# Low parts of block 0's FFN weights on GpSimd, the AV sum as one strided reduction, ten pair tiles, and a new order

## The chip, the cores and the metric

The kernel runs on one core of a Trainium2 chip. Its engines work side by side: TensorE (PE, matmuls; PEld are its weight loads), ScalarE (ACT), VectorE (DVE), GpSimd (POOL), and SyncE (SP), whose queue issues all transfers here. The metric is device time in microseconds (us), lower is better. The profile is of one execution; its span begins at the first and ends at the last recorded instruction.

## The reference

Everything is fp32; one sequence of 2048 positions, width 640, 32 heads of 20, FFN width 1728.

```python
H = 32; Dh = D // H; W, dil = 8, 2
qkv = (x @ wqkv)                       # x: layer-normed
idx = pos[:, None] - off[None, :]      # each position sees itself and 7 earlier ones, 2 apart
logits = jnp.einsum("bhsd,bhswd->bhsw", q, kg) * scale   # masked where idx < 0
attn = _softmax(logits, axis=-1)
o = jnp.einsum("bhsw,bhswd->bhsd", attn, vg)
h = x + o @ wo
g = _silu(ln(h) @ w_gate); u = ln(h) @ w_up
out = h + (g * u) @ w_down
```

## The kernel before

Positions are cut into four blocks of 512 (b = 0 to 3). Matmuls run on fp32r operands in three passes: each fp32 matrix is split into a high part (a rounded copy, made by ScalarE) and a low part (the rest, a subtraction), and high x high, low x high and high x low are added in PSUM. A low part is made by the helper `low`, on VectorE.

The stages are: QKV projections of all blocks (`qkv`, L691); attention on VectorE (`att_qk`, `att_exp`, `att_av`); output projection per block (`wo`, L888, and `wo3` for block 3, L1262); FFN of blocks 0 and 1 (`ffn`, `classic`: gate and up projections L976, down projections L991); FFN of blocks 2 and 3 together (`pair`), where a *pair tile* (`pair_tile`, L1164) takes a tile of 128 FFN columns through both blocks in a Winograd manner, 54 matmuls for what two classic tiles do in 2 x 30; at the end `products` (L1435), seven products in place of eight for the down projections of eight paired tiles.

The FFN has 14 tiles. `EARLY` says how many leading tiles blocks 2 and 3 take in the classic way (`ones` in `pair`, together with tile 13): with EARLY = 2 these are tiles 0, 1 and 13, eleven tiles are pair tiles, eight of those are *kept* for `products`. The classic tiles of block 2 are matmul work that does not need block 3, so it can run beside `wo3`.

Attention has 16 units (block, head group), two halves (`jp`) each. In a half, VectorE multiplies a window of keys with the queries into the buffer PROD (L755, 2560 elements per partition), reduces over the 20 head elements (L760), and later multiplies values with weights into PROD (L795), sums over the eight window places by halving three times in place (L804: 1280, 640, 320 elements), and transposes the result (L811). PROD is one buffer: each product waits for all readers of the one before.

The low parts of the FFN weights of block 0 are made by VectorE (`split`, L952: three subtractions of 640 per tile, from the loaded weights and their high parts, L957 and L942 on ScalarE), written to HBM (`lsc`) and loaded again for blocks 1 and 2. Products of FFN tiles come back through L1014 (ScalarE, silu), L1015 (VectorE, gate times up), L1005 and L1007 (split of the product), before the down matmuls.

The order of the work on each engine is not the program's: `Plan.add` records every operation with its reads and writes, and the table `ORDER`, worked out ahead by a planner from costs, says in which sequence the recorded operations are issued. Each row of it is (engine, number of the operation on that engine, how many). Every engine, SP's queue too, works its own sequence strictly in that order and waits by semaphores for what it needs from the others. `prio`, `cost` and `nbytes` in `P.add` have no effect beside a given `ORDER`.

GpSimd has little to do before the change: some memsets, among them empty operations that hold a place in the order.

Of the kernel before, what the change touches and what calls it, by code (L numbers as in the profile page):

```python
# [25 lines left out]
EARLY, NP = 2, 4  # L26
# [283 lines left out]
def dve(n):  # L310
    return 0.155 + 0.00104 * n
# [5 lines left out]
def pool(n):  # L317
    return 0.2 + 0.00218 * n
# [10 lines left out]
def program(tc, x_in, wqkv_in, wo_in, ffn_in, ffl_in, const_in, out):  # L329
# [8 lines left out]
    with tc.tile_pool(name="sb", bufs=1) as sb, tc.tile_pool(  # L338
# [107 lines left out]
        def low(n, fn, r, w, prio):  # L446
            P.add("DVE", dve(n), lambda: fn(V), r=r, w=w, prio=prio)
# [335 lines left out]
        def att_av(b, g, n, ko, vo, qo, lo, mo):  # L783
# [8 lines left out]
            for jp in range(2):  # L792
# [9 lines left out]
                def half(m, dst):  # L802
                    v = pq(PROD, 2560).rearrange("p (j w c) -> p j w c", j=2, w=W)
                    V.tensor_add(dst(v), v[:, :, 0:m, :], v[:, :, m : 2 * m, :])  # L804
# [833 lines left out]
```

## Time and profile before

| | us |
|---|---|
| median of 3 runs | 847.01 |
| lowest, highest | 845.8, 847.99 |
| profiled execution, its own time | 847.86 |
| its span | 845.8 |
| TensorE busy | 833.5 |
| VectorE busy | 753.7 |
| ScalarE busy | 431.9 |
| GpSimd busy | 2.8 |

The granted TensorE clock is 1.00 nearly throughout. Rows of groups give line, engine, operation, output<-input, shapes and count, then busy time and mean ns of one, then idle time of the engine just before and what ended it. Rows of waits give who waited for whom, us in total, times, longest.

### The profile page before, as it was taken

The page shows a single profiled execution, that of the slowest core. Times are in us where ns is not written, and L with a number is a line of the kernel's source. Part 1 is how long each engine was busy: PE and PEld are TensorE (multiplying, and loading weights), DVE is VectorE, ACT ScalarE, POOL GpSimd, SP SyncE. Part 2 cuts the span into 40 slices and gives each one's busy share as a digit, 9 for nine tenths or more (in the row PEclk, how much of TensorE's full clock was granted, in tenths as well). Part 3 has the DMA queues.
Part 4 walks back from the last instruction along what each step waited for, and adds up shares of the span by engine and source line. Part 5 has one row for each costly group of instructions (what it writes and reads, how often), then busy time and mean ns, then how long its engine had stood idle before and what let it go on. Part 6 is the DMA issues. An engine that isn't in the chain of part 4 may idle for free.

```text
span 845.8 us, 11075 instructions
## 1 busy us (share of the span) xinstructions
PE 833.5 (99%) x4037; PEld 713.4 (84%) x4037; DVE 753.7 (89%) x974; ACT 431.9 (51%) x804; POOL 2.8 (0%) x13
## 2 busy tenths in 40 slices
PE   8999999999999999999999999999999999999998
PEld 6888888889978788888888888888788888887998
DVE  6499999999998999999999999999986756667996
ACT  7755466253772443468345339467933232335550
POOL 0000000000000000000000000000000000000000
PEclk9999999999999999999999999999999999999999
DMA  7896978757779897679989989876322223268002
GB/s 256 224 246 172 283 203 236 217 142 227 187 216 282 271 283 235 222 218 275 328 265 299 283 278 283 247 268 241 120 90 75 88 82 100 81 227 323 1 33 93
DMA packets 89158, 173.35 MB, mean 205 GB/s; under 512 B 34464, under 2 KB 51200, under 8 KB 88464
## 3 DMA queue, kind: packets, MB, share of 16 engines
q1 hardware_dynamic: 89104, 172.66, 66.8%
q8 instruction: 31, 0.51, 0.2%
q14 instruction: 23, 0.19, 0.1%
HBM read 125.09 MB, written 47.16 MB: 204 GB/s over the span
## 4 chain that ended last, share of the span: by engine, by line
PE 78%; DVE 9%; DMA 8%; ACT 2%; issue 1%; SPq 1%; DVEq 0%; ACTq 0%
PE bank L691 18%; PE bank L976 18%; PE bank L1164 15%; PE bank L991 13%; PE bank L1435 6%; PE bank L888 5%; PE bank L1262 2%; DMA kv<-ksc 2%; DVE pq L795 1%; DMA pq<-qsc 1%; DMA vsc<-st 1%; DVE pq L755 1%; DMA lsc<-rb 1%; DVE rb L952 1%; DMA psc<-fa 1%
## 5 line engine op out<-in xcount | busy, mean ns | idle before, releaser
L976 PE MATMUL bank<-shb,rb 128*128 128x512 f32 x885 | 212.5, 390 | 1.9 <-DVE fa L1015 1.5
L976 PEld LDWEIGHTS bank<-shb,rb 128*128 128x128 f32 x885 | 165.1, 188 | 37.5 <-DVE fa L1015 2.4
L991 PE MATMUL bank<-rb,acts 128*128 128x512 f32 x464 | 122.5, 391 | 0.5 <-DVE acts L1009 0.5
L991 PEld LDWEIGHTS bank<-rb,acts 128*128 128x128 f32 x464 | 86.5, 188 | 18.4 <-DVE acts L1009 0.9
L755 DVE TENSOR_TENSOR pq<-kv,pq 128x2560 f32<-128x2560 f32 x32 | 90.2, 2820 | 6.4 <-DMA pq<-qsc 3.0
L804 DVE TENSOR_TENSOR pq<-pq 128x1280 f32<-128x1280 f32 (+2 forms) x96 | 89.4, 931 | 1.8
L795 DVE TENSOR_TENSOR pq<-kv,pq 128x2560 f32<-128x2560 f32 x32 | 90.2, 2820 | 0.7
L760 DVE TENSOR_REDUCE pq<-pq 128x128 f32<-128x2560 f32 x32 | 90.0, 2812 | 0.4
L698 ACT ACTIVATE st<-bank,fa 128x128 f32<-128x128 f32 (+3 forms) x120 | 50.5, 476 | 64.4 <-PE bank L691 37.7
L888 PE MATMUL bank<-ra 128*128 128x320 f32 x360 | 56.0, 309 | 0.0
L888 PEld LDWEIGHTS bank<-ra 128*128 128x128 f32 x360 | 54.3, 188 | 1.7 <-ACT fa L891 0.2
L691 PE MATMUL bank<-ra,sha 128*128 128x480 f32 (+2 forms) x240 | 54.4, 382 | 0.7 <-DVE sha L639 0.5
L691 PE MATMUL bank<-ra,shb 128*128 128x512 f32 (+1 forms) x240 | 52.5, 378 | 0.9 <-ACT st L698 0.9
L691 PE MATMUL bank<-rb,sha 128*128 128x512 f32 (+1 forms) x240 | 52.9, 379 | 0.0
L691 PE MATMUL bank<-rb,shb 128*128 128x512 f32 (+1 forms) x230 | 51.5, 379 | 0.0
L691 PEld LDWEIGHTS bank<-ra,shb 128*128 128x128 f32 x240 | 44.9, 188 | 7.8 <-ACT st L698 1.2
L691 PEld LDWEIGHTS bank<-ra,sha 128*128 128x128 f32 x240 | 44.3, 188 | 8.0 <-DVE sha L639 0.9
L691 PEld LDWEIGHTS bank<-rb,sha 128*128 128x128 f32 x240 | 44.8, 188 | 6.5
L691 PEld LDWEIGHTS bank<-rb,shb 128*128 128x128 f32 x230 | 42.9, 188 | 6.2
L957 ACT CAST rb<-fa 128x1280 fp32r<-128x1280 f32 (+1 forms) x32 | 38.9, 1215 | 17.9 <-DMA fa<-in_ffn_dram 14.4
L1014 ACT ACTIVATE fa<-bank 128x512 f32<-128x512 f32 x30 | 17.9, 598 | 51.1 <-PE bank L976 41.5
L952 DVE TENSOR_TENSOR rb<-fa,rb 128x640 fp32r<-128x640 f32 (+1 forms) x52 | 41.9, 814 | 1.1 <-ACT rb L957 1.1
(213 smaller groups left out, 1309.0 us busy)
## 6 DMA issues: line engine op xcount, KB each, us to landing
fa<-in_ffn_dram SPq DMA_DIRECT2D x33, 960.0 KB, 5.3
kv<-ksc SPq DMA_DIRECT2D x32, 440.0 KB, 6.2
kv<-vsc SPq DMA_DIRECT2D x32, 440.0 KB, 7.7
rb<-lsc SPq DMA_DIRECT2D x15, 640.0 KB, 6.4
lsc<-rb SPq DMA_DIRECT2D x13, 640.0 KB, 7.6
rb<-lsc SPq DMA_DIRECT2D x19, 320.0 KB, 4.4
ksc<-st SPq DMA_DIRECT2D x32, 160.0 KB, 3.5
pq<-qsc SPq DMA_DIRECT2D x16, 320.0 KB, 7.0
```

The lines of the kernel that those rows point to most:

```text
L691: T.matmul(banks[bk][:, 0:n], l, r_(wq(g, w, c) + shift, n), start=(p, c) == first_mm, stop=(p, c) == last_mm)
L698: P.add("ACT", act(m) + 0.06, lambda: A.activation(stage_t()[:, o : o + NJ * m].rearrange("p (t j c) -> p t j c", j=NJ, c=w)[:, :, j, :], ...
L755: P.add("DVE", dve(2560), lambda: V.tensor_tensor(pq(PROD, 2560).rearrange("p (j w c) -> p j w c", j=2, w=W), window(ko, 2 * jp), pq(qo + ...
L760: P.add("DVE", dve(2560), lambda: V.tensor_reduce(logits(lo)[:, :, 16 * jp : 16 * jp + 16].rearrange("p h n -> p n h"), pq(PROD, 2560).rea ...
L795: V.tensor_tensor(pq(PROD, 2560).rearrange("p (j n d) -> p j n d", j=2, d=DH), bass.AP(tensor=v.tensor, offset=v.offset, ap=[list(v.ap[0]) ...
L804: V.tensor_add(dst(v), v[:, :, 0:m, :], v[:, :, m : 2 * m, :])
L888: T.matmul(banks[bk][:, 0:320], l, r_(m, 320), start=p == 0 and c == 0, stop=p == 2 and c == NC - 1)
L952: low(640, lambda E, o=o: E.tensor_sub(ws(t, lo + o, 640)[p0:], fa[p0:, raw + o : raw + o + 640], ws(t, hi + o, 640)[p0:].bitcast(F32)), [ ...
L976: T.matmul(banks[bk], ws(wt, gu + 1280 * w + wid * c + col, 128), x(a, c), start=p == 0 and c == 0, stop=p == 2 and c == NC - 1)
L991: T.matmul(banks[k], l, m, start=first and p == 0, stop=stop and p == len(passes) - 1)
L1164: T.matmul(banks[bk], ws(wt, o + 2048 * w + 128 * k, 128), xv_[k](a), start=first and p == 0 and k == 0, stop=stop and p == 2 and k == n - ...
L1435: T.matmul(banks[bk0 + tp][:, 0:HN], v[:, 512 * a + 128 * tp : 512 * a + 128 * tp + 128], v[:, 1024 + HN * w : 1024 + HN * w + HN], start= ...
```

## The change

Four things change.

1. `low` gets a switch `aside`; `split` and `down_lo` pass it for block 0, so that the 41 subtractions of block 0's FFN weights are GpSimd's.
2. The AV sum, three halvings in PROD, becomes one VectorE reduction that reads PROD with the window place innermost (a step of 160 floats) and writes 320 sums into a free part of the query buffer; the transposition reads those.
3. After each of the 64 products a *token* is added on GpSimd: a copy of one element of PROD. It waits for the product, it does not hold back the reduction behind it, and the next product waits for it, since it reads PROD. In GpSimd's sequence it stands between the subtractions.
4. EARLY is 3: ten pair tiles in place of eleven, one classic tile more in block 2 and in block 3. The table `ORDER` is a new one.

```diff
-EARLY, NP = 2, 4
+EARLY, NP = 3, 4
...
 ORDER = (
-    (4, 2, 1), (4, 7, 1), (4, 4, 1), (2, 0, 1), (3, 1, 1), (3, 0, 1), (2, 1, 1), (1, 0, 1), (1, 10, 1), (2, 7, 1), (4, 3, 1), (2, 10, 1), (0, 0, 1), (4, 9, 1),
...
+    (4, 547, 1), (4, 552, 1), (4, 551, 1), (0, 833, 1), (2, 779, 1), (0, 828, 2), (2, 778, 1), (4, 546, 1), (4, 550, 1), (4, 549, 1),
...
-        def low(n, fn, r, w, prio):
-            P.add("DVE", dve(n), lambda: fn(V), r=r, w=w, prio=prio)
+        def low(n, fn, r, w, prio, aside=False):
+            if aside:
+                P.add("POOL", pool(n), lambda: fn(G), r=r, w=w, prio=prio)
+            else:
+                P.add("DVE", dve(n), lambda: fn(V), r=r, w=w, prio=prio)
...
+        def token():
+            P.add("POOL", 0.17, lambda: G.tensor_copy(f(LN + 122, 1), pq(PROD, 1)), r=[rpq(PROD, 1)], w=[rf(LN + 122, 1)], prio=20)
+
         def att_qk(jp, b, g, n, ko, vo, qo, lo, mo):
...
+            token()
             P.add("DVE", dve(2560), lambda: V.tensor_reduce(
...
-                def half(m, dst):
-                    v = pq(PROD, 2560).rearrange("p (j w c) -> p j w c", j=2, w=W)
-                    V.tensor_add(dst(v), v[:, :, 0:m, :], v[:, :, m : 2 * m, :])
-                for m in (4, 2):
-                    P.add("DVE", tt(320 * m), lambda m=m, half=half: half(m, lambda v: v[:, :, 0:m, :]),
-                          r=[rpq(PROD, 2560)], w=[rpq(PROD, 2560)], prio=20)
-                P.add("DVE", tt(320), lambda half=half: half(1, lambda v: v[:, :, 0:1, :]), r=[rpq(PROD, 2560)], w=[rpq(PROD, 2560)], prio=20)
...
+                token()
+                P.add("DVE", dve(2560), lambda: V.tensor_reduce(
+                    pq(qo + 256, 320).rearrange("p (j c) -> p j c", j=2), pq(PROD, 2560).rearrange("p (j w c) -> p j c w", j=2, w=W), axis=AX.X, op=ALU.add),
+                    r=[rpq(PROD, 2560)], w=[rpq(qo + 256, 320)], prio=20)
+                P.add("DVE", dve(320), lambda jp=jp: V.transpose(
+                    pq(oo + 320 * jp, 320).rearrange("p (f j t) -> p j f t", f=5, j=2), pq(qo + 256, 320).rearrange("p (j f t) -> p j f t", j=2, f=5)),
+                    r=[rpq(qo + 256, 320)], w=[rpq(oo + 320 * jp, 320)], prio=20)
...
-            split(wt, gu + 1280, raw, gu, n, 0)
-            down_lo(i, raw, n, dn)
+            split(wt, gu + 1280, raw, gu, n, 0, b == 0)
+            down_lo(i, raw, n, dn, b == 0)
```

Lines move by 2 to 4: L952 becomes L954, L976 L978, L991 L993, L1262 L1264, L1435 L1437, L760 L768, L755 L762, L795 L803. `bank_70` to `bank_77` are the eight PSUM banks 0 to 7, `rb` and `ra` hold weights, `shb`, `kv` normed inputs, `acts` FFN products, `pq` holds PROD.

*VectorE, late in block 0's FFN.* Before, a stretch with the two AV halves of a unit:

```order
L795 TENSOR_TENSOR pq<-kv,pq 128x2560
L952 TENSOR_TENSOR rb<-fa,rb 128x640
L1007 TENSOR_TENSOR acts<-fa,acts 128x512
L804 TENSOR_TENSOR pq<-pq 128x2x640
L1015 TENSOR_TENSOR fa<-bank_76,fa 128x512
L804 TENSOR_TENSOR pq<-pq 128x2x320
L894 TENSOR_TENSOR h<-h,fa 128x640
L804 TENSOR_TENSOR pq<-pq 128x2x160
L952 TENSOR_TENSOR rb<-fa,rb 128x640
L811 STREAM_TRANSPOSE pq<-pq 128x2x5x32
```

Now, the same stage:

```order
L803 TENSOR_TENSOR pq<-kv,pq 128x2560
L811 TENSOR_REDUCE pq<-pq 128x320
L803 TENSOR_TENSOR pq<-kv,pq 128x2560
L896 TENSOR_TENSOR h<-h,fa 128x640
L814 STREAM_TRANSPOSE pq<-pq 128x2x5x32
L811 TENSOR_REDUCE pq<-pq 128x320
L1009 TENSOR_TENSOR acts<-fa,acts 128x512
L1017 TENSOR_TENSOR fa<-bank_76,fa 128x512
L814 STREAM_TRANSPOSE pq<-pq 128x2x5x32
```

The subtractions are gone, and one reduction (L811) follows each product in place of three halvings.

*GpSimd, in the same stage.* Before there was one memset between the first and the last of these tiles; now, from the start of block 0's FFN, subtractions (L954) and tokens (L758):

```order
L758 COPY fa<-pq 128x1 x25
L954 TENSOR_TENSOR rb<-fa,rb 128x640 x2
L758 COPY fa<-pq 128x1
L954 TENSOR_TENSOR rb<-fa,rb 128x640
L758 COPY fa<-pq 128x1
L954 TENSOR_TENSOR rb<-fa,rb 128x640 x5
L1578 MEMSET acts 128x2
L954 TENSOR_TENSOR rb<-fa,rb 128x640
L758 COPY fa<-pq 128x1
L954 TENSOR_TENSOR rb<-fa,rb 128x640
L758 COPY fa<-pq 128x1
L954 TENSOR_TENSOR rb<-fa,rb 128x640 x3
```

Between two tokens stand one to six subtractions. Further on in this stage stand two more bursts, of five and of four.

*TensorE, at block 3's output projection.* Before:

```order
L1262 MATMUL bank_77<-ra 128x320 x9
L991 MATMUL bank_73<-rb,acts 128x512 x2
L1262 MATMUL bank_77<-ra 128x320 x18
L1262 MATMUL bank_70<-ra 128x320 x6
L1262 MATMUL bank_77<-ra 128x320 x9
L1262 MATMUL bank_70<-ra 128x320 x6
L1262 MATMUL bank_77<-ra 128x320 x6
L976 MATMUL bank_76<-shb,rb 128x512 x5
```

Now:

```order
L1264 MATMUL bank_77<-ra 128x320 x9
L978 MATMUL bank_75<-shb,rb 128x512 x5
L1264 MATMUL bank_77<-ra 128x320 x9
L978 MATMUL bank_75<-shb,rb 128x512 x5
L978 MATMUL bank_76<-shb,rb 128x512 x5
L1264 MATMUL bank_77<-ra 128x320 x9
L978 MATMUL bank_76<-shb,rb 128x512 x5
L1264 MATMUL bank_77<-ra 128x320 x9
L978 MATMUL bank_76<-shb,rb 128x512 x5
L1264 MATMUL bank_77<-ra 128x320 x9
```

Products into bank 7 stood next to each other; now projection groups of the extra classic tile of block 2 stand between them. In the whole stage these groups are eleven, where two were. At the start of the last products TensorE's order changes in the same manner: two groups of three of them (L1437) now stand before the last down group (L993), where none did.

More of the change, by code (lines that the diff above doesn't have):

```diff
@@ L800, in att_av @@
                 P.add("DVE", dve(2560), av, r=vr + [rpq(qo + 128 * jp, 128)], w=[rpq(PROD, 2560)], prio=20)
-                def half(m, dst):
-                    v = pq(PROD, 2560).rearrange("p (j w c) -> p j w c", j=2, w=W)
-                    V.tensor_add(dst(v), v[:, :, 0:m, :], v[:, :, m : 2 * m, :])
-                for m in (4, 2):
-                    P.add("DVE", tt(320 * m), lambda m=m, half=half: half(m, lambda v: v[:, :, 0:m, :]),
-                          r=[rpq(PROD, 2560)], w=[rpq(PROD, 2560)], prio=20)
-                P.add("DVE", tt(320), lambda half=half: half(1, lambda v: v[:, :, 0:1, :]), r=[rpq(PROD, 2560)], w=[rpq(PROD, 2560)], prio=20)
-                def turn(jp=jp):
-                    V.transpose(
-                        pq(oo + 320 * jp, 320).rearrange("p (f j t) -> p j f t", f=5, j=2),
-                        pq(PROD, 2560).rearrange("p (j w f t) -> p j w f t", j=2, w=W, f=5)[:, :, 0])
-                P.add("DVE", dve(320), turn, r=[rpq(PROD, 2560)], w=[rpq(oo + 320 * jp, 320)], prio=20)
+                token()
[5 more added lines that the diff above has]
+                    r=[rpq(qo + 256, 320)], w=[rpq(oo + 320 * jp, 320)], prio=20)
                 for q in range(4) if (b, g, jp) != (NB - 1, NG - 1, 1) else ():
@@ L942, in down_hi, with down_lo @@
             P.add("ACT", act(640), lambda: A.copy(r_(dn[0], 640), f(raw + n, 640)), r=[rf(raw + n, 640)], w=[rr(dn[0], 640)], prio=PR["fh"])
-        def down_lo(i, raw, n, dn):
+        def down_lo(i, raw, n, dn, aside=False):
             last = i == NF - 1
@@ L947, in down_lo, with split @@
                 P.add("POOL", 1.0, lambda: G.memset(r_(dn[1], 640)[0:64].bitcast(F32), 0.0), w=[rr(dn[1], 640)], prio=PR["fh"])
-            split(0, dn[1], raw + n, dn[0], 640, 64 if last else 0)
-        def split(t, lo, raw, hi, n, p0):
+            split(0, dn[1], raw + n, dn[0], 640, 64 if last else 0, aside)
+        def split(t, lo, raw, hi, n, p0, aside=False):
             for o in range(0, n, 640):
                 low(640, lambda E, o=o: E.tensor_sub(ws(t, lo + o, 640)[p0:], fa[p0:, raw + o : raw + o + 640], ws(t, hi + o, 640)[p0:].bitcast(F32)),
-                    [rf(raw + o, 640), rws(t, hi + o, 640)], [rws(t, lo + o, 640)], PR["fl"])
+                    [rf(raw + o, 640), rws(t, hi + o, 640)], [rws(t, lo + o, 640)], PR["fl"], aside)
         def load_ffn(b, i, wt, gu, dn):
```

465 rows, old and new, of the table ORDER are left out of this document.

## The prediction

> **What bounds the kernel now.** I read the page first: span, then the busy row of each engine.
>
> ```profile
> span 845.8 us, 11075 instructions
> PE 833.5 (99%) x4037; PEld 713.4 (84%) x4037; DVE 753.7 (89%) x974; ACT 431.9 (51%) x804; POOL 2.8 (0%) x13
> ```
>
> TensorE is busy 99%, VectorE 89%, GpSimd not at all. A table of busy time by stage, cut where the kernel's stages change, shows where each is short (first number: the length; then busy time of PE, PEld, DVE, ACT, POOL; granted clock, DMA share, GB/s):
>
> ```profile
> 0.00:25.00 25.00, 21.62 (x97) 17.51 (x98) 16.08 (x40) 18.47 (x41) 1.17 (x7) 1.00 0.76 259
> 25.00:225.00 200.00, 199.14 (x974) 174.62 (x973) 185.42 (x180) 109.29 (x253) 0.00 (x0) 1.00 0.78 212
> 225.00:300.00 75.00, 72.08 (x338) 60.65 (x338) 70.68 (x76) 39.35 (x63) 0.10 (x1) 1.00 0.87 257
> 300.00:550.00 250.00, 249.93 (x1195) 211.60 (x1194) 246.21 (x256) 132.92 (x207) 0.63 (x1) 1.00 0.87 267
> 550.00:625.00 75.00, 74.03 (x365) 62.24 (x364) 71.93 (x143) 52.42 (x101) 0.10 (x1) 1.00 0.53 186
> 625.00:750.00 125.00, 125.00 (x553) 103.39 (x552) 81.04 (x129) 39.99 (x64) 0.69 (x2) 1.00 0.28 95
> 750.00:800.00 50.00, 49.17 (x236) 41.20 (x236) 43.92 (x75) 23.82 (x45) 0.10 (x1) 1.00 0.55 198
> 800.00:846.00 46.00, 42.50 (x290) 42.24 (x288) 38.42 (x80) 15.66 (x34) 0.00 (x0) 0.99 0.15 58
> ```
>
> VectorE is nearly full from 225 to 625 us, because the attention runs there beside the projections and FFNs of other blocks. But it does not set the time: in 300 to 550 it works 246.2 of 250 us and TensorE still 249.9 of 250. What VectorE does too late shows only as TensorE's few holes, and these bound the gain. Outside the first and the last stage TensorE is idle 0.86 + 2.92 + 0.07 + 0.97 + 0 + 0.83 = 5.65 us. Busy time hides some of a hole, since matmul ends are modelled; the waits of TensorE's weight loads, which stand ahead of its matmuls, name the holes better:
>
> ```profile
> PEld bank L976 <- DVE fa L1015: 3.2, 3, 1.9
> PEld bank L1262 <- ACT fa L1272: 2.0, 5, 0.8
> PEld bank L548 <- ACT st L698: 1.4, 1, 1.4
> PEld bank L691 <- ACT st L698: 1.2, 1, 1.2
> PEld bank L991 <- DVE acts L1009: 0.9, 1, 0.9
> PEld bank L1164 <- DVE rb L1129: 0.7, 1, 0.7
> PEld bank L1164 <- issue: 0.5, 1, 0.5
> ```
>
> So everything that a lighter VectorE or a better order can win lies in some ten microseconds, however many VectorE microseconds are freed.
>
> **Six matmuls more (a cost).** EARLY 3 turns one pair tile, 54 matmuls for blocks 2 and 3 together, into an ordinary tile of each, 2 x 30. The rate comes from the chain of waits, in order of time, where TensorE runs unbroken (start, us, count):
>
> ```profile
> 724.61 25.85 PE bank L1164 x114
> ```
>
> 25.85/114 = 0.227 us each, so 6 x 0.227 = **+1.4 us** on the engine that is full. Nothing covers it. The rest of this swap is small and lies where there is room: the tile's weights are loaded once more and its kept product is neither stored nor loaded (same count of transfers in all, DMA share 0.28 from 625 us), and what VectorE does for one tile changes in a stage where it works 81 of 125 us: 0.
>
> **What VectorE gives up.** In 225 to 420 us the low parts of block 0's FFN weights are (instructions of one line, duration min/median/max, first and last start):
>
> ```profile
> L952 DVE TENSOR_TENSOR rb<-fa,rb x41: 779/815/822, 236.0 to 397.9; 128x640 fp32r<-128x640 f32 x40, 64x640 fp32r<-64x640 f32 x1
> ```
>
> 41 x 0.815 = 33.4 us go to GpSimd. The AV sum's three halvings become one reduction over 2560 elements. These are VectorE's groups (busy, mean ns of one):
>
> ```profile
> L755 DVE TENSOR_TENSOR pq<-kv,pq 128x2560 f32<-128x2560 f32 x32 | 90.2, 2820 | 6.4 <-DMA pq<-qsc 3.0 <-DMA kv<-ksc 2.7 <-DMA fa<-in_ffn_dram 0.5
> L760 DVE TENSOR_REDUCE pq<-pq 128x128 f32<-128x2560 f32 x32 | 90.0, 2812 | 0.4
> L804 DVE TENSOR_TENSOR pq<-pq 128x1280 f32<-128x1280 f32 x32 | 47.6, 1487 | 0.6
> L804 DVE TENSOR_TENSOR pq<-pq 128x640 f32<-128x640 f32 x32 | 26.2, 820 | 0.5
> L804 DVE TENSOR_TENSOR pq<-pq 128x320 f32<-128x320 f32 x32 | 15.6, 486 | 0.6
> ```
>
> The halvings take 1487 + 820 + 486 = 2793 ns. No row has the new reduction: it reads one float, jumps 160 floats (640 bytes), reads the next. Its lower end is L760, the same operation on as many elements, read in sequence: 2812 ns, +0.02 x 32 = +0.6 us in all. Its upper end comes from the only row with a wide stride, ScalarE's copy that writes 8 floats apart (L781), beside an operation of the same size in sequence (L780):
>
> ```profile
> L781 ACT COPY pq<-pq 128x256 f32<-128x256 f32 x16 | 11.2, 699 | 0.3
> L780 ACT ACTIVATE pq<-pq 128x256 f32<-128x256 f32 x16 | 6.7, 419 | 7.6 <-DVE pq L779 7.5
> ```
>
> (699 - 419)/256 = 1.1 ns per element, which would make the reduction 2812 + 2560 x 1.1 = 5.6 us and cost 32 x 2.83 = 90 us of VectorE. I take the lower end, since L760 is the same engine, operation and count and reads, while L781 is another engine's write; the upper end is a rival and widens the range. The Trainium skill speaks against me here: "SBUF — State Buffer", in the note on cachelines under "Door 1: The DMA port swizzle", says that an access that leaves a 16-byte line each time pays a penalty. It gives no figure, L781 agrees with it, L760 cannot test it; by it the sum is that of the rival below.
>
> So VectorE has about 33 us less in 236 to 571 us. Attention's last transposition (L811):
>
> ```profile
> L811 DVE STREAM_TRANSPOSE pq<-pq x32: 497/511/514, 67.3 to 571.6; 128x320 f32<-128x320 f32 x32
> ```
>
> The output projection of block 3 that waits for it follows at once, by the chain of waits (start, us, count):
>
> ```profile
> 572.40 5.54 PE bank L1262 x36
> ```
>
> VectorE's end moves up by about 30 us, while that part moves back by the extra tile's 30 + 15 matmuls, 45 x 0.227 = 10 us: 40 us of cover where there was almost none.
>
> **What GpSimd takes on.** 41 subtractions of 640 elements and 64 tokens. Bounds from its row of that length, and a row for the least an instruction takes:
>
> ```profile
> L947 POOL MEMSET rb<- 64x640 f32 x2 | 1.3, 626 | 139.9 <-PE bank L991 139.9
> L1576 POOL MEMSET acts<- 128x2 f32 x1 | 0.1, 101 | 253.1 <-DMA ksc<-st 253.1
> ```
>
> A write alone takes 0.63 us, two reads and a write one after another at most 3 x 0.63 = 1.9 us: 26 to 78 us within 162 us, so GpSimd can keep up on average; I take 1.5, nearer the end with all three streams. The Trainium skill, "GPSIMD Engine Reference", 3.1, gives 4497 ns for 2048 elements, an estimated 1.4 us here; no run shows it yet. A token waits for the product before it, and the next product waits for the token, since both use PROD. Behind a token that is late stand all later lows, and the matmuls that need them; behind lows that are late stands the next token, and so VectorE's next product. Normally the 2.8 us reduction between two products hides a token (some 0.1 us, as L1576) and one low.
>
> **Where the holes go.** Output projection of block 3: before, groups on bank 77 stand close together, each waiting for ScalarE's eviction, with two projection groups among them. Afterwards eleven projection groups stand between. The waits L1262 and both L1164 are 2.0 + 0.7 + 0.5 = 3.2 us; a load's wait overlaps up to 0.2 us of streaming, so I take **-2.6**. At the end, where one part of the last products now goes ahead of the down groups, stand the 0.9 us of L991 and, in 750 to 800 us,
>
> ```profile
> PEld bank L976 <- DVE fa L1015: 0.7, 1, 0.7
> ```
>
> together 1.6, of which I take **-1.3**. In block 0's FFN the L976 waits that are left, 3.2 - 0.7 = 2.5 us, come when VectorE's gate product stands behind attention and two lows. The lows go, the attention stays, and a late load of keys (2.7 us in L755's row) stands there too: I take **-1.0**. The start (L548, L691, ScalarE and transfers) has no reason to change: 0, with 1 us either way for the shuffled first matmuls.
>
> Sum: +1.4 - 2.6 - 1.3 - 1.0 = -3.5 us. The profiled execution took 847.86 us for its span of 845.8, so 2.1 us lie around the span and stay. That execution is 0.85 over the median of 847.01; from the median the forecast is **843.5 us**, its own range 841.5 to 847.
>
> **Rivals.**
> *Scattered reads at L781's price (slower).* One mechanism at one place: each of the 32 new reductions takes up to 2.8 us more. VectorE then has 90 + 0.6 - 33.4 = 57 us more before 571 us, of which its idle time in 225 to 550 (4.3 + 3.8) absorbs some 8, and the later place of block 3's projection some 10. TensorE would wait about 40 us, about half of it already at block 0's FFN (8 reductions, 23 us late, and no other matmuls are left there): 885 us. Against it speaks L760, for it L781. It decides from about 1 us per reduction, where 32 x 1 us eat the 33 freed; at half L781's price only block 0's start is late, by 8 x 1.4 = 11 us before its own slack, some 855 us.
> *GpSimd and VectorE in each other's way.* In GpSimd's order three to six lows stand between two tokens four times: at five, 5 x 1.5 = 7.5 us against a product and a reduction of 5.6, so the next product comes 2 us late; four such bursts are 8 us of VectorE, less than it was given. But lows that come late hold matmuls: 14 tiles at 0.5 us are 7 us of TensorE, so 847 + 1.4 + 7 - 3.9 (the holes after 550 us) = 851.5 us. For it: the two engines meet in one buffer, and GpSimd's queue is strict. Against: at 41 x 1.5 = 62 of 162 us GpSimd is loaded little over a third. The Trainium skill, "SBUF — State Buffer", "Who interferes with whom", has a reason for it: a VectorE operation with two SBUF inputs and a GpSimd one that reads SBUF exclude each other for the whole instruction, a reduction does not. The trace of before, where GpSimd reads nothing beside VectorE, cannot show it; by that rule lows outside reductions cost VectorE up to their own length.
> *The holes do not close.* New places for the same waits; only the six matmuls are left: 848.4 us, no change. For it: VectorE was full in 300 to 550 us and TensorE did not notice, so freeing VectorE there need not be noticed either.
>
> **Chances.** Forecast 0.45, holes stay 0.20, in each other's way 0.17, scattered reads 0.18. About 0.3% (2.5 us) can be told from no change. Of the forecast's 0.45 some 0.36 lies below 844.5; with a little from the second, faster 0.38; same 0.31 (the rest of the forecast, the holes that stay, a mild second rival); slower 0.31. The range takes in the second rival and a scattered read at up to half its price: 840 to 862 us.
>
> **What would show it.** The new reduction's mean ns (2.8 or up to 5.6) decides the first rival. Right: VectorE's last transposition of attention near 540 us, no TensorE wait on ScalarE's eviction at block 3's projection, no wait at the start of the products. Wrong: weight-load waits on GpSimd between 240 and 400 us, VectorE idle until a token, GpSimd's subtractions far over 1.9 us, products of 2.82 us grown longer.

## The result: 7.2% slower

The changed kernel takes 907.77 us (906.66 to 908.43, median of 4 runs) against 847.10 us (845.80 to 847.99, 4 runs) for the kernel before on the same chip: a ratio of 1.0721, 95% interval 1.0704 to 1.0738, or +61 us. Every ratio in this document is of undisturbed executions; one execution of e6 below, 921.2 us at a granted clock of 0.85, is left out by this. The forecast was 843.5 us, its range ended at 862.

The page of the changed kernel: span, busy row, and the groups that answer to those of the prediction (busy, mean ns of one, idle time before).

```profile
span 904.9 us, 11130 instructions
PE 854.8 (94%) x4043; PEld 726.8 (80%) x4043; DVE 800.8 (88%) x859; ACT 430.6 (48%) x800; POOL 89.9 (10%) x118
L811 DVE TENSOR_REDUCE pq<-pq 128x320 f32<-128x2560 f32 x32 | 155.8, 4870 | 0.9
L803 DVE TENSOR_TENSOR pq<-kv,pq 128x2560 f32<-128x2560 f32 x32 | 92.7, 2896 | 2.7 <-DMA kv<-vsc 1.0
L768 DVE TENSOR_REDUCE pq<-pq 128x128 f32<-128x2560 f32 x32 | 89.9, 2810 | 0.4
```

The new reduction (L811) takes 4870 ns where the three halvings took 2793. The old reduction (L768), on as many elements read in sequence, still takes 2810. VectorE was to become 33 us lighter and is 47 us busier.

Busy time by stage of the changed kernel (length; busy time of PE, PEld, DVE, ACT, POOL; granted clock, DMA share, GB/s):

```profile
25.00:225.00 200.00, 190.62 (x905) 165.97 (x904) 183.16 (x136) 96.42 (x220) 5.57 (x22) 0.97 0.69 197
225.00:300.00 75.00, 64.08 (x299) 53.77 (x298) 69.47 (x54) 41.09 (x80) 21.74 (x19) 0.95 0.72 195
300.00:550.00 250.00, 234.05 (x1072) 195.70 (x1071) 237.58 (x178) 113.56 (x174) 58.62 (x58) 0.97 0.80 245
```

TensorE, nearly full before, is idle 9.4, 10.9 and 16.0 us in these stages, in the projections from 25 us on already. Its waits name VectorE's work for the matmuls (us in total, times, longest): the gate product L1017, its split L1009, the normed inputs L556.

```profile
PE bank L978 <- DVE fa L1017: 13.5, 7, 4.4
PE bank L993 <- DVE acts L1009: 8.4, 4, 2.5
PE bank L552 <- DVE shb L556: 7.0, 2, 6.0
```

**Where the 59 us of span went.** Attention's last transposition starts at 636.1 us (571.6 before):

```profile
L814 DVE STREAM_TRANSPOSE pq<-pq x32: 493/507/516, 79.1 to 636.1; 128x320 f32<-128x320 f32 x32
```

Cut at its end, the kernel before and then the changed one:

```profile
0.00:225.00 225.00, 220.77 (x1069) 192.13 (x1070) 201.50 (x220) 127.75 (x293) 1.17 (x7) 1.00 0.78 217
225.00:572.10 347.10, 343.85 (x1645) 290.56 (x1644) 338.67 (x360) 185.36 (x291) 0.73 (x2) 1.00 0.86 264
```

```profile
0.00:225.00 225.00, 212.19 (x999) 183.38 (x1000) 200.40 (x177) 115.52 (x261) 6.73 (x29) 0.98 0.70 204
225.00:636.60 411.60, 379.20 (x1746) 317.04 (x1744) 392.49 (x299) 197.91 (x322) 82.23 (x85) 0.97 0.79 237
```

VectorE works 592.9 us up to there, against 540.2: +52.7. It is idle 43.7 us, against 31.9: +11.8. Together attention ends 64.5 us later. What follows takes 904.9 - 636.6 = 268.3 us, against 845.8 - 572.1 = 273.7: 5.4 us less. 64.5 - 5.4 = 59.1 us, the whole difference of the spans. So the question is what makes VectorE's attention longer.

### The profile page after: what moved, and what is told of

It reads as the page before. It is cut to its first block, busy times and chain, and to the rows that moved or that the text cites. A ratio compares the mean times of both kernels' runs of the same rounds, so it can differ in the third digit from the quotient of the medians.

```text
span 904.9 us, 11130 instructions
## 1 busy us (share of the span) xinstructions
PE 854.8 (94%) x4043; PEld 726.8 (80%) x4043; DVE 800.8 (88%) x859; ACT 430.6 (48%) x800; POOL 89.9 (10%) x118
## 5 line engine op out<-in xcount | busy, mean ns | idle before, releaser
L978 PE MATMUL bank<-shb,rb 128*128 128x512 f32 x915 | 231.1, 399 | 13.7 <-DVE fa L1017 13.5
L978 PEld LDWEIGHTS bank<-shb,rb 128*128 128x128 f32 x915 | 174.4, 193 | 52.7 <-DVE fa L1017 14.1
L811 DVE TENSOR_REDUCE pq<-pq 128x320 f32<-128x2560 f32 x32 | 155.8, 4870 | 0.9
L993 PE MATMUL bank<-rb,acts 128*128 128x512 f32 x464 | 125.0, 394 | 2.2 <-DVE acts L1009 2.1
L993 PEld LDWEIGHTS bank<-rb,acts 128*128 128x128 f32 x464 | 87.3, 190 | 20.9 <-DVE acts L1009 3.0
L803 DVE TENSOR_TENSOR pq<-kv,pq 128x2560 f32<-128x2560 f32 x32 | 92.7, 2896 | 2.7 <-DMA kv<-vsc 1.0
L762 DVE TENSOR_TENSOR pq<-kv,pq 128x2560 f32<-128x2560 f32 x32 | 91.0, 2843 | 1.9 <-DMA pq<-qsc 1.6
L768 DVE TENSOR_REDUCE pq<-pq 128x128 f32<-128x2560 f32 x32 | 89.9, 2810 | 0.4
L954 POOL TENSOR_TENSOR rb<-fa,rb 128x640 fp32r<-128x640 f32 (+1 forms) x41 | 70.2, 1726 | 47.4 <-ACT rb L944 18.9
L702 ACT ACTIVATE st<-bank,fa 128x480 f32<-128x480 f32 (+3 forms) x120 | 49.9, 473 | 48.7 <-PE bank L695 26.4
L758 POOL COPY fa<-pq 128x1 f32<-128x1 f32 x64 | 17.7, 276 | 490.2 <-DVE pq L762 242.5
L890 PE MATMUL bank<-ra 128*128 128x320 f32 x360 | 59.4, 319 | 3.7 <-ACT ra L879 2.0
L890 PEld LDWEIGHTS bank<-ra 128*128 128x128 f32 x360 | 56.7, 196 | 6.6 <-ACT ra L879 2.2
```

The source lines that it names most:

```text
L702: P.add("ACT", act(m) + 0.06, lambda: A.activation(stage_t()[:, o : o + NJ * m].rearrange("p (t j c) -> p t j c", j=NJ, c=w)[:, :, j, :], ...
L762: P.add("DVE", dve(2560), lambda: V.tensor_tensor(pq(PROD, 2560).rearrange("p (j w c) -> p j w c", j=2, w=W), window(ko, 2 * jp), pq(qo + ...
L768: P.add("DVE", dve(2560), lambda: V.tensor_reduce(logits(lo)[:, :, 16 * jp : 16 * jp + 16].rearrange("p h n -> p n h"), pq(PROD, 2560).rea ...
L803: V.tensor_tensor(pq(PROD, 2560).rearrange("p (j n d) -> p j n d", j=2, d=DH), bass.AP(tensor=v.tensor, offset=v.offset, ap=[list(v.ap[0]) ...
L811: P.add("DVE", dve(2560), lambda: V.tensor_reduce(pq(qo + 256, 320).rearrange("p (j c) -> p j c", j=2), pq(PROD, 2560).rearrange("p (j w c ...
L890: T.matmul(banks[bk][:, 0:320], l, r_(m, 320), start=p == 0 and c == 0, stop=p == 2 and c == NC - 1)
```

## The experiments

The three parts of the change that can be set one by one are the AV sum (three halvings or the strided reduction), who makes the 41 low parts of block 0 (VectorE or GpSimd), and the order of the work (the one before with eleven pair tiles, or the new one with ten). All eight combinations were run. Each ratio is to the kernel before on the same chip:

| AV sum | low parts | order | label | us | ratio, 95% interval |
|---|---|---|---|---|---|
| halvings | VectorE | before | the kernel before | 845.31 to 847.10 | 1 |
| halvings | GpSimd | before | e10 | 854.26 | 1.0104 [1.0085, 1.0122] |
| halvings | VectorE | new | e3 | 856.76 | 1.0122 [1.0091, 1.0153] |
| halvings | GpSimd | new | e1 | 864.87 | 1.0213 [1.0174, 1.0251] |
| strided | VectorE | before | e9 | 918.55 | 1.0838 [1.0815, 1.0860] |
| strided | GpSimd | before | e12 | 912.27 | 1.0783 [1.0755, 1.0812] |
| strided | VectorE | new | e2 | 914.40 | 1.0815 [1.0798, 1.0832] |
| strided | GpSimd | new | the change | 907.77 | 1.0721 [1.0704, 1.0738] |

The tokens are in every row with the new order and in none with the order before.

### The strided sum undone (e1)

```diff
-                P.add("DVE", dve(2560), lambda: V.tensor_reduce(
-                    pq(qo + 256, 320)..., pq(PROD, 2560).rearrange("p (j w c) -> p j c w", j=2, w=W), axis=AX.X, op=ALU.add), ...)
+                def tree():
+                    v = pq(PROD, 2560).rearrange("p (j w c) -> p j w c", j=2, w=W)
+                    for m in (4, 2):
+                        V.tensor_add(v[:, :, 0:m, :], v[:, :, 0:m, :], v[:, :, m : 2 * m, :])
+                    V.tensor_add(pq(qo + 256, 320)..., v[:, :, 0:1, :], v[:, :, 1:2, :])
+                P.add("DVE", dve(2560), tree, ...)
```

> The changed kernel with the AV sum as three halvings again (the last one writes to the query buffer, as the reduction did; the token reads an element that the halvings don't write); GpSimd's subtractions, ten pair tiles and the new order stay. Theory scattered read: the strided reduction's 4.87 us against 2.79 for the halvings, 32 x 2.08 = 67 us of VectorE, made the loss; without it 844 to 852 us. Rival, GpSimd's coupling (subtractions and tokens in one strict queue, and two-input VectorE operations shut out): the time stays above 880 us, since the halvings have two SBUF inputs and would be shut out more often.

Measured 864.87 us, above the theory's 844 to 852 and below the rival's 880: the strided reduction is 43 of the 61 us in this kernel, and 18 us remain.

### The strided sum alone, in the order before (e9)

```diff
-                for m in (4, 2):
-                    P.add("DVE", tt(320 * m), lambda m=m, half=half: half(m, ...), ...)
-                P.add("DVE", tt(320), lambda half=half: half(1, ...), ...)
+                P.add("DVE", dve(2560), lambda: V.tensor_reduce(
+                    pq(qo + 256, 320)..., pq(PROD, 2560).rearrange("p (j w c) -> p j c w", j=2, w=W), axis=AX.X, op=ALU.add), ...)
```

> The kernel before in its own order, with one thing changed: the three halvings of the AV sum become one reduction that reads PROD with a step of 160 floats and writes beside the queries (five transfers, those of query rows that this place would collide with, are issued a little later). Theory (the strided read alone is the large cost): a reduction takes 4.5 to 4.9 us in place of 2.79 us of halvings, VectorE gets 32 x 1.7 to 2.1 = 54 to 67 us more with nothing freed, and TensorE waits for most of it: 885 to 900 us. Rival (the strided sum was dear only beside GpSimd's subtractions and in the new order, and here VectorE's slack and the later FFN absorb it): under 865 us.

Measured 918.55 us, above the theory's 885 to 900 and far from the rival's 865. The two reductions of this kernel side by side:

```profile
L747 DVE TENSOR_REDUCE pq<-pq 128x320 f32<-128x2560 f32 x32 | 154.8, 4837 | 0.6
L702 DVE TENSOR_REDUCE pq<-pq 128x128 f32<-128x2560 f32 x32 | 90.1, 2814 | 0.4
```

32 x (4837 - 2793) = 65 us more of VectorE cost 72 us of time. Nothing absorbed them. The strided sum alone is dearer than the whole change.

### What a jump costs (probe)

The kernel before, with these operations added behind its end, where nothing else runs, in one execution: VectorE reductions of 2560 elements to 320, reading 1, 2, 4, 8, 32 or 160 floats apart (L1609 to L1614); VectorE products that write 1, 2, 4, 8 or 160 floats apart (L1616 to L1620, the second and third shown); ScalarE copies in sequence, writing 8 apart, reading 8 apart (L1622 to L1624); and five GpSimd subtractions of 640 elements (L1629) beside each of four VectorE operations: a reduction in sequence, a strided one (L1633), a product of two SBUF operands (L1634), a product with one operand in PSUM.

> The kernel before, with operations added behind its end that its result does not use: VectorE reductions of 2560 elements to 320 with steps of 1, 2, 4, 8, 32 and 160 floats, products written with steps of 1, 2, 4, 8 and 160 floats, ScalarE copies that read or write 8 floats apart, and five GpSimd subtractions of 640 beside four VectorE operations each (reduction in sequence, reduction with step 160, product with two SBUF inputs, product with one PSUM input). Scattered read: reductions near 2.81 us up to a step of 2 floats and near 4.9 from 8 on. If the step is not the cause, all reductions take 2.81. Shut out: the two-input product and GpSimd's subtraction beside it each take longer than alone, the reductions and the PSUM product do not.

Groups (busy, mean ns of one, idle before):

```profile
L1609 DVE TENSOR_REDUCE fa<-fa 128x320 f32<-128x2560 f32 x3 | 8.5, 2817 | 0.1
L1610 DVE TENSOR_REDUCE fa<-fa 128x320 f32<-128x2560 f32 x3 | 8.5, 2820 | 0.1
L1611 DVE TENSOR_REDUCE fa<-fa 128x320 f32<-128x2560 f32 x3 | 14.1, 4684 | 0.1
L1614 DVE TENSOR_REDUCE fa<-fa 128x320 f32<-128x2560 f32 x3 | 13.4, 4452 | 0.1
L1617 DVE TENSOR_TENSOR fa<-fa 128x2560 f32<-128x2560 f32 x3 | 8.5, 2825 | 0.1
L1618 DVE TENSOR_TENSOR fa<-fa 128x2560 f32<-128x2560 f32 x3 | 14.1, 4691 | 0.1
L1622 ACT COPY fa<-fa 128x2560 f32<-128x2560 f32 x3 | 7.0, 2325 | 141.1 <-DVE fa L1627 141.0
L1624 ACT COPY fa<-fa 128x2560 f32<-128x2560 f32 x3 | 14.4, 4787 | 0.1
```

A step of 2 floats is free (2820); a step of 4 floats, 16 bytes, costs 1.87 us per reduction (4684), and a step of 160 floats no more (4452). Writes behave the same (2825 at 2, 4691 at 4), and so does ScalarE (2325 in sequence, 4787 when it reads 8 apart). That is what the Trainium skill, "SBUF — State Buffer", says in the note on cachelines under "Door 1: The DMA port swizzle": an access needs at least two hits on a 16-byte line for full speed, and each crossing to a new line pays. Steps 2 and 4 lie on the two sides of just that bound; where the same note of the Trainium skill counts 4 fp32 as a stride that is free, the measurement decides, since a step of 4 pays in full. The price here is (4452 - 2817)/2560 = 0.64 to (4684 - 2817)/2560 = 0.73 ns per element on VectorE and (4787 - 2325)/2560 = 0.96 on ScalarE.

The probe's second part, as a timeline (start, us, engine, line, count): four products of two SBUF operands beside four of the five GpSimd subtractions.

```profile
1039.45 15.04 DVE L1634 TENSOR_TENSOR fa<-fa 128x2560 f32<-128x2560 f32 x4
1039.52 16.36 POOL L1629 TENSOR_TENSOR fa<-fa 128x640 f32<-128x640 f32 x4 [10.06 <-DVE fa L1627]
```

Four products alone would take 4 x 2.825 = 11.3 us and four subtractions 4 x 1.54 = 6.2 us, 17.5 one after another; side by side they need 16.4, so they take turns. All subtractions, the strided reductions beside them, and these products (duration min/median/max):

```profile
L1629 POOL TENSOR_TENSOR fa<-fa x20: 1529/1543/4147, 974.1 to 1064.1; 128x640 f32<-128x640 f32 x20
L1633 DVE TENSOR_REDUCE fa<-fa x4: 4451/4484/4542, 1021.4 to 1035.0; 128x320 f32<-128x2560 f32 x4
L1634 DVE TENSOR_TENSOR fa<-fa x4: 2826/4036/4036, 1039.5 to 1050.5; 128x2560 f32<-128x2560 f32 x4
```

The strided reduction stays at 4484 and most subtractions at 1543; the product of two SBUF operands goes from 2826 (the shortest) to 4036, and the subtractions beside it to as much as 4147. The product with one operand in PSUM (L1635) takes 686 to 693 ns beside the last five subtractions, as long as such products take in the kernels (L1015, 680). This is the rule of the Trainium skill, "SBUF — State Buffer", "Who interferes with whom", that the prediction cites under its second rival; here the trace agrees.

### The jump moved from the read to the write (e4)

The product is written 8 floats apart and the sum then reads in sequence:

```diff
-                        pq(PROD, 2560).rearrange("p (j n d) -> p j n d", j=2, d=DH),
+                        pq(PROD, 2560).rearrange("p (j h d w) -> p j w h d", j=2, h=8, d=DH),
...
-                    ... pq(PROD, 2560).rearrange("p (j w c) -> p j c w", j=2, w=W), axis=AX.X, op=ALU.add)
+                    ... pq(PROD, 2560).rearrange("p (j c w) -> p j c w", j=2, w=W), axis=AX.X, op=ALU.add)
```

> The changed kernel, but the product of values and weights is written so that the eight window places stand side by side (VectorE writes 8 floats apart), and the reduction reads in sequence. Scattered read, price for reads alone: product stays 2.82 us, reduction 2.81, time 844 to 852 us. If a scattered write costs as ScalarE's did (1.1 ns per element more), the product takes about 5 us and the time stays at 890 to 910. GpSimd's coupling: above 880 us with a reduction of 2.81 us.

Measured 922.43 us, ratio 1.0900 [1.0864, 1.0937], above the 890 to 910 expected for a write that pays. The sum is cheap again and the product pays, as that branch of the expectation had it:

```profile
L743 DVE TENSOR_TENSOR pq<-kv,pq 128x2560 f32<-128x2560 f32 x32 | 166.7, 5211 | 1.9 <-DMA kv<-vsc 0.3
L751 DVE TENSOR_REDUCE pq<-pq 128x320 f32<-128x2560 f32 x32 | 90.1, 2817 | 0.9
```

The jump cannot be hidden by moving it to the other side. The probe's product at the same step takes 4748 ns. Of the 32 here, the six that a GpSimd subtraction overlaps take 5593 on average, the other 26 still 5122; so meeting GpSimd explains only a small part of the difference, and the busy TensorE of the last section is the likely rest.

### The low parts on GpSimd, with halvings (e8, e10) and with the strided sum (e2, e12)

e8 and e10 are the kernel before with `aside` for block 0 (e8 only for the 27 low parts of the gate and up weights, which its expectation misstates as 41; e10 for all 41):

```diff
+        def low(n, fn, r, w, prio, aside=False):
+            if aside:
+                P.add("POOL", pool(n), lambda: fn(G), r=r, w=w, prio=prio)
...
-            split(wt, gu + 1280, raw, gu, n, 0)
-            down_lo(i, raw, n, dn)
+            split(wt, gu + 1280, raw, gu, n, 0, b == 0)
+            down_lo(i, raw, n, dn, b == 0)
```

> The kernel before in its own order, with halvings and without tokens; only the 41 low parts of block 0's FFN weights go to GpSimd, at the same places in the order. Theory A (exclusion): VectorE is freed of 33 us, and its two-input operations beside the subtractions grow by 1.0 to 1.2 us for each subtraction that meets one, about as much in all; the time is the same or a little longer, 846 to 851 us. Theory B (what cost 8 us in the changed order was the order, and the freed VectorE closes the waits of block 0's FFN): 844 to 846 us. Theory C (late subtractions hold the matmuls at once): above 853 us.

> The kernel before in its own order with all 41 low parts on GpSimd. In the run before it, whose expectation says 41, only the 27 of the gate and up weights were moved, and the 14 of the down weights stayed on VectorE (855.2 us, +8.6). Theory (exclusion: a price for each subtraction beside two-input operations, 8.6/27 = 0.32 us of the end each): 41 x 0.32 = 13 us, 857 to 862 us. Rival (only the early gate and up parts hold matmuls; the down parts are needed later): 853 to 856 us.

Measured 855.22 us, ratio 1.0099 [1.0082, 1.0117], for 27 of them, and 854.26 us for all 41. The move alone makes the kernel 8 to 9 us slower. e8's time is in theory C's range, but not by C's mechanism: TensorE's waits in e8 name no subtraction, they name VectorE's gate product,

```profile
PE bank L918 <- DVE fa L957: 5.1, 3, 2.4
```

so what shows is A's mechanism at a higher price. In e10 the rival's number came: the down parts add nothing, the price is not so much per subtraction. The stretch from 225 to 425 us (length, busy time of PE, PEld, DVE, ACT, POOL, as above) and VectorE's groups in it, before and then in e10:

```profile
225.00:425.00 200.00, 197.01 (x939) 166.24 (x939) 194.17 (x214) 106.31 (x168) 0.73 (x2) 1.00 0.85 258
L804 DVE TENSOR_TENSOR pq<-pq 128x1280 f32<-128x1280 f32 x10 | 14.8, 1484 | 0.1
L1007 DVE TENSOR_TENSOR acts<-fa,acts 128x512 fp32r<-128x512 f32 x14 | 9.4, 673 | 0.0
```

```profile
225.00:425.00 200.00, 191.45 (x906) 159.31 (x905) 197.04 (x169) 103.94 (x163) 92.32 (x43) 1.00 0.79 246
L702 DVE TENSOR_REDUCE pq<-pq 128x128 f32<-128x2560 f32 x10 | 28.1, 2809 | 0.1
L746 DVE TENSOR_TENSOR pq<-pq 128x1280 f32<-128x1280 f32 x10 | 21.3, 2126 | 0.2
L949 DVE TENSOR_TENSOR acts<-fa,acts 128x512 fp32r<-128x512 f32 x14 | 18.4, 1312 | 0.0
```

VectorE has lost some 32 us of low parts and is no lighter (194.2 and 197.0 us), and TensorE works 5.6 us less: the halving grew from 1484 to 2126 ns, the split of the FFN product (L1007, now L949), on which the down matmuls wait, from 673 to 1312. The one-input reduction (L702) did not move (2807 before).

With the strided sum the same move helps:

> The changed kernel (strided reduction, tokens, new order, 907.8 us) with one thing undone: the 41 low parts are VectorE's again, at the same places in the order, so VectorE has 33 us more. Theory (beside the strided kernel too, what VectorE gave to GpSimd it paid back in two-input operations that have to wait): no large difference, 903 to 915 us. Rival (the move relieves VectorE, now that VectorE sets the pace and its reductions, with one input, leave GpSimd alone): 920 to 940 us.

> The kernel before in its own order, with the strided reduction (918.6 us alone) and all 41 low parts on GpSimd (854.3 us alone, +8); no tokens, eleven pair tiles. Theory (a strided reduction has one input and leaves GpSimd alone for 4.8 us, so that part of the freed 33 us is kept, as in the changed order, where the move was worth 914.4 - 907.8 = 6.6 us): 906 to 916 us. Rival (the price of the move, +8 us, is the same beside any attention): 922 to 930 us.

e2 (the change with `aside` taken out again) takes 914.40 us, e12 (e9 with the edit of e10) 912.27. Moving the low parts to GpSimd wins 6.6 us in the new order (914.40 to 907.77) and 6.3 in the order before (918.55 to 912.27), or 8 and 5 us by the ratios, which leave out the difference between chips; with halvings it costs 8. A strided reduction is a one-input operation 4.9 us long, beside which the probe's subtractions ran undisturbed; three halvings are all two-input ones. The busy rows of the pages show what VectorE keeps of the 33 us that it gave up: nothing with halvings (753.7 before, 764.3 in e10; 751.0 in e3, 754.0 in e1), some 7 and 15 us with the strided sum (818.7 in e9, 811.7 in e12; 816.0 in e2, 800.8 in the change). The rest is paid back there too, in the products and splits, which have two inputs. e2's time still lies in its theory's range, whose words ("no large difference") were wide; its rival had the direction and at least twice the size. e12, written with e2's result known, came out as its theory said.

### Seven low parts behind key products (e11)

Seven low parts, each right behind a key product in GpSimd's order, meant to run beside the reduction over the head elements; the rest as in the kernel before:

```diff
+            if len(P.ops) in ASIDE:
+                def beside():
+                    G.tensor_copy(f(LN + 122, 1), pq(PROD, 1))
+                    fn(G)
+                P.add("POOL", dve(n), beside, r=r, w=w, prio=prio)
```

> The kernel before in its own order, with 7 of the 41 low parts on GpSimd, each of them put right behind a key product of the attention and led by a copy of one element of PROD on GpSimd, so that it runs while VectorE reduces over the head elements (one input, 2.8 us long); the other 34 stay on VectorE. Theory (only two-input operations exclude GpSimd): the subtractions take 1.5 to 1.6 us, VectorE's products stay at 2.82 us and VectorE is 7 x 0.8 = 5.7 us lighter; 845 to 847 us, the same or a little faster. Rival (any subtraction on GpSimd costs, by its length and the waits between the engines): +0.3 us for each or more, 848.5 to 851 us.

Measured 848.91 us, ratio 1.0038 [1.0024, 1.0051]: the rival's number, +3.2 us. But the edit did not do all that it was meant to do. In the trace only the subtractions at 267, 305 and 343 us run beside that reduction; the other four meet operations with two inputs. The seven, and two of the lines that they met (duration min/median/max):

```profile
L898 POOL TENSOR_TENSOR rb<-fa,rb x7: 1568/1572/3465, 267.3 to 390.2; 128x640 fp32r<-128x640 f32 x7
L725 DVE TENSOR_TENSOR pq<-pq x16: 416/425/1730, 55.9 to 548.5; 128x256 f32<-128x256 f32 x16
L840 DVE TENSOR_TENSOR h<-h,fa x8: 783/818/1981, 338.1 to 518.3; 128x640 f32<-128x640 f32 x8
```

The longest of L725 and of L840 are the ones beside a subtraction; with L733 (1001 for 417) and L470 (1421 for 161) VectorE pays back 4.3 us, of 7 x 0.81 = 5.7 that it gave up. Its busy time is 753.5 us, against 753.7 before. The reductions beside the other three stay at 2810 to 2815 ns. So the theory about the operations holds, but its 5.7 us did not come, and this run does not test what a move that meets no two-input operation is worth. The profiled execution, 0.8 us of span over the kernel before, has no new wait that would explain +3.2 us, so that stays open. No version here beats the kernel before.

### The order and the tokens (e3, e6, e7)

e3 is e1 with the low parts on VectorE again; e6 is e3, and e7 is e1, without the tokens:

```diff
-            P.add("POOL", 0.17, lambda: G.tensor_copy(f(LN + 122, 1), pq(PROD + 1000, 1)), r=[rpq(PROD + 1000, 1)], ...)
+            P.add("POOL", 0, lambda: None)
```

> As the run before, and the 41 subtractions are VectorE's again, at the same places of the order; tokens, ten pair tiles and the new order stay. Scattered read: 846 to 856 us, within some us of the run with GpSimd's subtractions, VectorE 33 us fuller. GpSimd's coupling: this run alone falls to 850 us or less, and is at least 20 us faster than the run before.

> The kernel with halvings, with the low parts on VectorE again, and with the 64 tokens taken out (856.8 us with them, against 846.6 for the kernel before). Theory (the places in the new order cost, since the low parts stand on VectorE where the order had them on GpSimd, in front of the gate products): no change, 855 to 858 us. Rival (the tokens, 0.67 us each, hold VectorE's next product): 64 tokens that delay VectorE by a part of their length would give back up to 10 us, 847 to 851 us.

> The changed kernel with halvings in place of the strided reduction, low parts on GpSimd, and the 64 tokens taken out, so that GpSimd does a subtraction as soon as its weights are there (864.9 us with tokens). Theory (what costs is that a GpSimd subtraction and a VectorE operation with two SBUF inputs exclude each other, whenever it comes): within 3 us, 862 to 868 us, subtractions still near 1.9 us, halvings and products still longer than in the kernel before. Rival (the tokens make the subtractions late, and the matmuls wait for those): 850 to 858 us.

e3 took 856.76 us, just above its first theory's 846 to 856 and 8 us under e1, not the 20 of its second. e6 has a ratio of 1.0112 [1.0085, 1.0140] against e3's 1.0122, and e7 863.71 us, 1.0196 [1.0178, 1.0214], against e1's 1.0213. So 8 us come back when the low parts return to VectorE, as the price of the move in the order before; and with halvings the tokens cost nothing that can be measured, within some 2 us, as the theories of e6 and e7 had it. What is left, some 10 us with the low parts on either engine (e3 against before, e1 against e10), is the new order with its ten pair tiles, whose six matmuls more are 1.4 us of it. In e3 most of the rest is lost in block 0's FFN:

```profile
225.00:300.00 75.00, 69.72 (x311) 56.80 (x310) 71.89 (x79) 36.98 (x54) 5.91 (x9) 0.98 0.79 227
300.00:425.00 125.00, 120.71 (x572) 100.77 (x571) 119.52 (x133) 61.05 (x98) 9.29 (x14) 0.99 0.81 247
```

TensorE is idle 5.3 + 4.3 us from 225 to 425, where before it was idle 2.9 + 0.1: 6.6 us more, at a clock of 0.98 and 0.99. From 550 to 625, where it was idle 1.0 us before, it is full. With the strided sum the new order costs nothing: 1.0815 against 1.0838 with the low parts on VectorE, which can hardly be told apart, and 1.0721 against 1.0783 with them on GpSimd, where it wins. Which places in the order lose the 10 us was not taken apart.

## Why the prediction was wrong

**The step that failed is in "What VectorE gives up": the reduction's price.** Between L760 (2812 ns) and L781's price per element (5.6 us) it took the lower end, since L760 is the same engine, operation and count. But L760 reads in sequence: it shares everything with the new reduction except the one property in question, as the text itself said ("L760 cannot test it"). L781, another engine and a write, shares that property, and the probe shows that both engines pay, and on VectorE reads and writes alike. The term was to be +0.6 us and is 32 x (4870 - 2793) = +66 us. This alone turned 33 us less into 33 us more of VectorE.

**The first rival had the mechanism and its sign; its sizes erred twice, in opposite directions.** Its price was too high, 2.8 us per reduction against 2.1. With 2.1 its own arithmetic would have given 33 us more of VectorE, less some 8 of slack and 10 for block 3's later projection: about 15 us, 862 us. What happened is +61. The slack did not absorb anything: VectorE's idle time up to the end of attention grew from 31.9 to 43.7 us, since it now waits for the others in turn (its longest waits up to 636.6 us, of which the kernel before has 0.2 and 0.7):

```profile
DVE shb L556 <- ACT shb L555: 13.2, 4, 11.3
DVE fa L1017 <- PE bank L978: 7.7, 4, 3.1
```

Engines with strict orders that hand work to each other add their delays. The later projection gave 5.4 us, not 10. And 19 of VectorE's 52.7 us more are neither the sum (66.4) nor the low parts (-32.9). Operations with two inputs grew by 13: the two kinds of products by 3.3, the split L1009 by 26 x (808 - 672) = 3.5, smaller ones by some 6. The other 6 us are overlap that is gone: in the trace most operations begin a little before the one ahead of them ends, so 474 of them in place of 579 overlap less. Their durations add up to 46.3 us more (570.9 to 617.2), the busy time to 52.7. The rival's slack also carries its figure of some 855 us for a half price, which no run tests; e9 lost 72 us for 65 us of VectorE.

**"What GpSimd takes on": a subtraction's own time was right, its effect was not.** The changed kernel's 41, and their median:

```profile
L954 POOL TENSOR_TENSOR rb<-fa,rb x41: 1543/1578/4152, 248.8 to 432.9; 128x640 fp32r<-128x640 f32 x40, 64x640 fp32r<-64x640 f32 x1
```

1.58 us against the 1.5 taken. A token (L758) takes 276 ns on average, not 0.1 us, which with halvings did not matter (e7). **The second rival** had the right engines for the wrong reason: its bursts between tokens cost nothing measurable (e7, with halvings), while the mechanism that it cited beside them, that a two-input VectorE operation and a GpSimd one exclude each other and a reduction does not, is what the probe and e10 show, and it costs 8 to 9 us with halvings. In the change itself the move won 6 to 8 us (e2), since the strided sum leaves GpSimd alone.

**"Where the holes go" was right on block 3's projection and wrong on the end and on block 0.** With the attention's cost back in place (e3), the 3.2 us of weight-load waits at block 3's projection and the start of the pair tiles are 1.1. At the end stood 1.6 us, and one wait of nearly that size is left, on ScalarE's silu, where the forecast had -1.3:

```profile
PEld bank L922 <- ACT fa L960: 1.3, 1, 1.3
```

In block 0's FFN, where the forecast had -1.0, TensorE is idle 6.6 us longer. The prediction looked at what stood in front of the L976 waits in the old order, and not at what the new one put in front of the matmuls there. The six matmuls are there (4043 against 4037). The third rival, that nothing changes, fails like the forecast.

## What to carry to other kernels

Price a strided access by a row that strides, however unlike it is otherwise: here the same operation in sequence misled by 73%, and ScalarE's copy was nearer. Three halvings in sequence beat one reduction that steps 16 bytes or more at every element. A GpSimd subtraction leaves one-input VectorE operations as they are and lengthens two-input ones, so what a move to GpSimd is worth depends on what runs beside it, and parts of a change that cost 72, 9 and 10 us alone may cost 61 together.

## What the runs showed of the hardware beyond that

**A strided read takes longer beside a busy TensorE, one in sequence does not.** The strided reduction takes 4452 ns alone (probe) and 4837 on average inside e9. Two of them there, one beside a nearly idle and one beside a full TensorE (timeline), then the same stretches with their busy times and that of a third, of 4.83 us:

```profile
600.31 4.50 DVE L747 TENSOR_REDUCE pq<-pq 128x320 f32<-128x2560 f32 x1
550.30 4.89 DVE L747 TENSOR_REDUCE pq<-pq 128x320 f32<-128x2560 f32 x1
```

```profile
600.30:604.80 4.50, 0.65 (x3) 0.19 (x1) 4.49 (x2) 0.00 (x0) 0.00 (x0) 0.99 0.95 262
550.30:555.20 4.90, 4.90 (x28) 4.41 (x27) 4.90 (x3) 2.69 (x4) 0.00 (x0) 1.00 0.71 281
559.80:564.60 4.80, 4.54 (x26) 3.78 (x24) 4.79 (x2) 0.00 (x0) 0.00 (x0) 1.00 0.34 94
```

The one beside three matmuls takes 4.50 us, the one beside 28 takes 4.89, though the DMA share is the higher one beside the first (0.95 against 0.71). ScalarE, busy beside the second only, is not the cause: it stands still beside the third. Over all 32 the duration goes with TensorE's busy share (correlation 0.94) and hardly with ScalarE's (0.19). The reduction in sequence takes 2814 inside e9 and 2817 alone: it does not notice. This is read from the trace and was not tried by itself, and matmuls and weight loads were not told apart.

**A hole in TensorE's work can cost more than its length.** The changed kernel around 120 us, in stretches of 2 us (116 to 118 left out):

```profile
114.00:116.00 2.00, 2.00 (x12) 1.85 (x11) 2.00 (x2) 0.00 (x0) 0.00 (x0) 1.00 1.02 267
118.00:120.00 2.00, 0.73 (x4) 0.25 (x2) 2.00 (x1) 0.37 (x1) 0.00 (x0) 1.00 1.16 234
120.00:122.00 2.00, 0.78 (x2) 0.63 (x3) 2.00 (x4) 0.47 (x1) 0.58 (x1) 0.87 0.59 176
122.00:124.00 2.00, 2.00 (x6) 1.57 (x5) 2.00 (x1) 1.94 (x6) 0.00 (x0) 0.50 0.69 195
```

After 2.5 us without matmuls (118.7 to 121.2) the granted clock is 0.50 and the busy TensorE does 6 matmuls in 2 us, where it did 12 before the hole. In this execution twelve holes are longer than 1.9 us. With ten of them comes a stretch of 3.4 us, once 6.8, at a clock of 0.50; with two (2.1 us at 283, 2.35 us at 560) comes none, nor with the three holes of about 1.5 us, so what decides it is open. The ten stretches, 37.5 us in all, are why the stages of the change show clocks of 0.95 to 0.97, where the kernel before has 1.00, and why busy time understates the loss: TensorE is busy 854.8 us against 833.5, 21 us more, for six matmuls more, which are 1.4.
